# Spectral layer, soft mixture of experts and SoLU on one core: the turned slot weights kept slot-major, and the products with w_sb in another order

## The chip, the cores and the metric

The kernel runs on one core of a Trainium2 chip. The metric is the device time of one execution in microseconds; three runs of the kernel before took 1307.14, 1307.5 and 1311.27 us, and their median is 1307.5 us.

## The reference

All data are fp32. Three layers follow each other:

```
X = rfft(x, axis=1)                    # x: 8 batches x 3072 positions x 256
Yr, Yi = complex product of X with w_r, w_i, plus b_r, b_i
Yr, Yi = soft threshold at 0.01        # sign(y) * max(|y| - 0.01, 0)
x = irfft(Yr + i Yi)                   # flattened to 24576 x 256
logits = x @ phi                       # 32 slots
d = softmax of logits over all 24576 rows, c = softmax over the 32 slots
slot_input = d.T @ x                   # 32 x 256
slot_out = relu(slot_input @ w1[e]) @ w2[e]   # 8 experts, 4 slots each
x = c @ slot_out
h = x @ w_in; solu = h * softmax(h); ln = layernorm(solu) * g_ln
out = ln @ w_out
```

## The kernel before

The first stage (phase1) goes through the 8 batches. For each it transforms x, multiplies it with the weights of the frequencies (mix), thresholds, and keeps the result s in the frequency domain: 12 tiles of 128 x 512 per batch. The rows of the inverse transform are never formed. Because the transform is linear, logits and slot inputs are computed from s: the logits are the inverse transform of s @ phi (qt, qtr, e2, r_x, inv1), and the slot input of a batch is the forward transform of the weights d, multiplied with s.

That forward transform of d is the part that changes. Its steps for batch b are:

- fwd1 (two halves h): 16 small products per half give dt, 128 partitions (4 column groups l times 32 slots) by 8 x 4 x 32.
- dtr (two halves): four TensorE transposes of 128 x 128 per half write one PSUM tile, and ScalarE copies it to dm_sb, whose free axis is (position, l, slot).
- d_x (two halves z of 16 slots): VectorE's transpose of 32 x 32 blocks, dm_sb to dm2_sb, 128 x 512 each; input and output are read and written with the slot axis outermost and steps of 32 floats inside.
- fwd2: for each half c, products with w_sb (the tile w2_sb, 128 x 64 of it) into one PSUM tile of 128 x 384: columns of the array 0 to 63 write partitions 0 to 63, columns 64 to 127 write 64 to 127. The 32 columns of q = 0, t = 0 take another weight. ScalarE copies the tile to dh_sb.
- slots: 24 products of dh_sb with s, four column groups at a time, accumulate the slot input of the batch; acc takes it over the batches.

The order of the work is written out by hand. The main loop goes over the 96 tiles (b, t) and issues, for each, stage1 of a later tile, stage2 of the next one, st_transpose and mix. The steps above stand in a heap with a number of ticks behind their predecessor (LAG, and FAST for batch 6) and are issued between these parts, four ticks per tile. So each engine's queue is fixed when the kernel is built. Steps of a batch run while later tiles are being transformed. fwd2 of batches 0 to 6 is issued in this loop. For batch 7 nothing is left to run beside them, and the function last_chain writes its steps out one behind the other, with some filler matmuls on TensorE (run_on).

After it the second stage (phase2) computes the experts' outputs (first, turns, second) with weights that are loaded while last_chain runs, and then goes over 192 tiles of 128 rows: h, softmax, layer norm, and the product with w_out.

The helper mm issues every product (L89), tp every transpose (L92). An fp32 product is two matmul records and two weight loads in the trace, a transpose is one of each. In the names of the trace dm2_sb shows as dm_sb, r2_sb as r_sb, and the weight w2_sb as w_sb. The weight loads of inv_mm (r2, step of 32 floats) and of fwd_mm (d, contiguous), and the transposes in turns (h1, step of 8 floats) are read in the prediction beside the changed lines.

Of the kernel before, what the change touches and what calls it, by code (L numbers as in the profile page):

```python
# [13 lines left out]
AF = mybir.ActivationFunctionType  # L14
# [21 lines left out]
def kernel(  # L36
# [25 lines left out]
    PE, ACT, DVE, POOL, SP = nc.tensor, nc.scalar, nc.vector, nc.gpsimd, nc.sync  # L62
# [25 lines left out]
    def mm(out, lhsT, rhs, start=True, stop=True):  # L88
        PE.matmul(out=out, lhsT=lhsT, rhs=rhs, start=start, stop=stop)  # L89

    def tp(out, in_, k=128):
        PE.transpose(out=out, in_=in_, identity=ident[0:k, 0:k])  # L92
# [53 lines left out]
    def phase1(pl: ExitStack, pr_: ExitStack):  # L146
# [21 lines left out]
        w2_sb = ks_p.tile([128, 2, 2, 64], F32, name="w2_sb")  # L168
# [16 lines left out]
        def after(dq, fn, *a):  # L185
            heapq.heappush(heap, (now[0] + dq, now[1], fn, a))
            now[1] += 1
# [3 lines left out]
        def lag(name, b):  # L191
            return FAST[name] if b == B - 2 else LAG[name]
# [183 lines left out]
        small = {}  # L376
# [3 lines left out]
        def sm(name, shape, n=1):  # L380
            return sm_p.tile(shape, F32, name=name, tag=share.get(name, name), bufs=n)

        def pm(shape):
            return (small["pool"] if "pool" in small else psm).tile(shape, F32, name="pm", tag="pm")
# [71 lines left out]
        def r_x(b, z):  # L456
            if z == 0:
                small["r2", b] = sm("r2_sb", [128, 32, 32])
            sl = slice(16 * z, 16 * z + 16)
            DVE.transpose(out=small["r2", b][:, sl], in_=r_sb[:, sl])  # L460
            if z and b == B - 1:
                last_chain(b)
            elif z:
                after(lag("inv1", b), inv1, b, 0)
                after(lag("inv1", b) + 1, inv1, b, 1)

        def last_chain(b):
# [3 lines left out]
            dt = small["dt", b] = sm("dt_sb", [128, 8, 4, 32])  # L471
            POOL.memset(dt[:, :, :, 24:32], 0.0)
            pl_ = []
            for h in range(2):
                ps = pm([128, 4, 96])
# [14 lines left out]
            for h in range(2):  # L490
                ps = pm([96, 4, 128])
# [14 lines left out]
            for h in range(2):  # L506
                ps = pm([128, 4, 4, 24])
                fwd_mm(ps, d, h)
                ACT.activation(out=dt[:, 4 * h:4 * h + 4, :, 0:24], in_=ps, func=AF.Copy, scale=m3[:, 1 + h:2 + h])
            c = sm("c_sb", [96, 32, 32])  # L510
            rm, rs = sm("rm", [96, 32, 1]), sm("rs", [96, 32, 1])
            dm = small["dm", b] = sm("dm_sb", [128, 8, 128])
            for h in range(2):
                ps = pm([128, 4, 128])
                for k in range(4):
                    tp(ps[:, k, :], dt[:, 4 * h + k].rearrange("p c g -> p (c g)"))
                ACT.activation(out=dm[:, 4 * h:4 * h + 4, :], in_=ps, func=AF.Copy)
            lg = []
            for h in range(2):
                ps = psm.tile([96, 4, 128], F32, name="pm", tag="pm")  # L520
# [19 lines left out]
            DVE.tensor_scalar(out=srun, in0=srun, scalar1=m3[:, 0:1], scalar2=None, op0=ALU.mult)  # L540
            DVE.tensor_scalar(out=acc, in0=acc, scalar1=m3[:, 0:1], scalar2=None, op0=ALU.mult)
            d_x(b, 0)
            d_x(b, 1)
            for z in half:
                DVE.tensor_reduce(out=rm[:, z], in_=lg[z.start // 16], op=ALU.max, axis=AX.X)
                csub(z)
            fwd2(b)
            for z in half:
                cexp(z)
# [161 lines left out]
        def fwd1(b, h):  # L711
            if h == 0:
                small["dt", b] = sm("dt_sb", [128, 8, 4, 32])
                POOL.memset(small["dt", b][:, :, :, 24:32], 0.0)
            d, dt = small["d", b], small["dt", b]
            ps = pm([128, 4, 4, 24])
            fwd_mm(ps, d, h)
            ACT.activation(out=dt[:, 4 * h:4 * h + 4, :, 0:24], in_=ps, func=AF.Copy)
            after(LAG["dtr"], dtr, b, h)

        def dtr(b, h):
            if h == 0:
                small["dm", b] = sm("dm_sb", [128, 8, 128])
            dt, dm = small["dt", b], small["dm", b]
            ps = pm([128, 4, 128])
            for k in range(4):
                tp(ps[:, k, :], dt[:, 4 * h + k].rearrange("p c g -> p (c g)"))
            ACT.activation(out=dm[:, 4 * h:4 * h + 4, :], in_=ps, func=AF.Copy)
            if h == 1:
                after(lag("d_x", b), d_x, b, 0)  # L730
                after(lag("d_x", b) + 1, d_x, b, 1)

        def d_x(b, z):
            if z == 0:
                small["dm2", b] = sm("dm2_sb", [128, 32, 32])
            sl = slice(16 * z, 16 * z + 16)
            dm = small["dm", b].rearrange("p a (l s) -> p (a l) s", l=4)
            DVE.transpose(out=small["dm2", b].rearrange("p g s -> p s g")[:, sl], in_=dm.rearrange("p n s -> p s n")[:, sl])
            if z and b < B - 1:
                after(lag("fwd2", b), fwd2, b)  # L740

        def fwd2(b):
            dm2 = small["dm2", b][:, 0:24].rearrange("p (q g t) s -> p q g (t s)", q=3, g=2)
            dh = sm("dh_sb", [128, 2, NT, 32])
            for c in range(2):
                ps = pm([128, 3, 128])
                mm(ps[0:64, 0, 0:32], w2_sb[:, 1, c, :], dm2[:, 0, 0, 0:32])
                mm(ps[64:128], w2_sb[:, 0, c, :], dm2[:, :, 1, :])
                mm(ps[0:64, 0, 32:128], w2_sb[:, 0, c, :], dm2[:, 0, 0, 32:128])
                mm(ps[0:64, 1:3], w2_sb[:, 0, c, :], dm2[:, 1:3, 0, :])  # L750
                ACT.activation(out=dh[:, c].rearrange("p t s -> p (t s)"), in_=ps.rearrange("p q j -> p (q j)"), func=AF.Copy)
                small["dh", b] = dh
                if b == B - 1 and c == 0:
                    sums4(b)
            if 0 < b < B - 1:
                DVE.tensor_scalar(out=acc, in0=acc, scalar1=mexp[:, 0:1], scalar2=None, op0=ALU.mult)
            if b < B - 1:
                after(LAG["sums4"], sums4, b)
                after(LAG["slots"], slots, b)
# [37 lines left out]
        def sums4(b):  # L797
            s4 = sm("s4", [1, 4, 32])
            ACT.activation(out=s4, in_=small["dh", b][0:1, 0, 0:1, :].to_broadcast([1, 4, 32]), func=AF.Copy, scale=float(N))
            small["s4"] = s4  # L800
            if b < B - 1:
                after(LAG["sums"] + 2, sums, b, s4)
# [152 lines left out]
        for k in range(0, 8, 2):  # L955
            z = slice(128 * k, 128 * k + 256)
            decs.append((w_out[z].rearrange("(k p) d -> p k d", p=128), None, k))

        for i in range(B * NT):
            b, t = divmod(i, NT)  # L960
# [3 lines left out]
            if i + 1 < B * NT:  # L964
                stage2(*divmod(i + 1, NT))
                if t % 2 == 0:
                    k = i // 2 + 2
# [10 lines left out]
            if quiet:  # L978
                fn, a = quiet.pop(0)
# [9 lines left out]
        while heap or quiet:  # L989
            if quiet:  # L990
                fn, a = quiet.pop(0)
# [445 lines left out]
    with tc.manual_schedule():  # L1437
        with ExitStack() as ps_, ExitStack() as pl, ExitStack() as pw:
            s_p = ps_.enter_context(tc.tile_pool(name="s_p", bufs=NS))
            wa_p = pw.enter_context(tc.tile_pool(name="wa_p", bufs=2, side="right"))  # L1440
            g_p = pw.enter_context(tc.tile_pool(name="g_p", bufs=1, side="right"))
            gl = g_p.tile([128, 8], F32, name="gl")
            gm = g_p.tile([128, 1, D], F32, name="gm")
            with ExitStack() as pr_:
                steps = phase1(pl, pr_)
                next(steps)
            wb_p = pw.enter_context(tc.tile_pool(name="wb_p", bufs=15, side="right"))
            wi_p = pw.enter_context(tc.tile_pool(name="wi_p", bufs=1, side="right"))
            psg = pw.enter_context(tc.tile_pool(name="psg", bufs=1, space=PSUM, side="right"))
            wi = wi_p.tile([128, 2, DFF], F32R, name="wi")  # L1450
            load_w(wb_p, "wb", 15)
            SP.dma_start(out=wi.bitcast(F32), in_=win_dram.rearrange("(k p) f -> p k f", p=128))
            for _ in steps:
                pass
            pl.close()
            with ExitStack() as p2:
                phase2(p2, pw)
# [122 lines left out]
```

## Time and profile before

| | |
|---|---|
| median of three runs | 1307.5 us (1307.14 to 1311.27) |
| profiled execution | 1307.97 us, span 1306.2 us |
| granted TensorE clock, mean | 0.993 |
| busy: TensorE, VectorE, GpSimd, ScalarE | 97%, 86%, 77%, 76% |
| first stage | until about 597 us |
| tiles of the second stage | from about 622 us |

A group row of the profile gives line, engine, operation, the tiles written and read, the shape and the count. PE stands for TensorE's matmuls, PEld for its weight loads, DVE for VectorE, ACT for ScalarE, POOL for GpSimd, SP for the queue that issues most transfers. The duration of a matmul in the trace holds the way through the array as well, so matmuls that follow each other overlap in the trace; their rate is read from start to start.

### The profile page before, as it was taken

What the parts mean: (1) busy time and instruction counts of PE and PEld (TensorE: products, weight loads), DVE (VectorE), ACT (ScalarE), POOL (GpSimd) and SP (SyncE); (2) the same over time, 40 slices, a digit from 0 to 9 for tenths busy, and PEclk for the clock granted to TensorE, in tenths of its full rate; (3) what the DMA queues carried; (4) which work ended last, traced back from release to release, by engine and by line L of the source; (5) the groups of instructions that cost most, each with busy time, mean ns of one, the idle gap of its engine ahead of it and who ended that gap; (6) DMA issues with size and microseconds to landing.
All of it is one profiled execution on the core that took longest, in us unless ns stands there. A gap on an engine that the chain in (4) does not pass through costs nothing.

```text
span 1306.2 us, 30976 instructions
## 1 busy us (share of the span) xinstructions
PE 1263.1 (97%) x11042; PEld 1115.7 (85%) x11042; DVE 1127.9 (86%) x1568; ACT 988.0 (76%) x1831; POOL 1010.7 (77%) x1114
## 2 busy tenths in 40 slices
PE   6989999999999999899699999999999999999998
PEld 2867878787878878865699999999999999999998
DVE  1867887888788888765999999999999999999995
ACT  3545556565656565543799999999999999999996
POOL 0868686877778775433589999999999999998995
PEclk8999999999999999999999999999999999999999
DMA  8986465564747364259467777777777787777874
GB/s 269 279 229 191 125 176 165 142 198 122 203 118 223 100 200 144 93 186 351 99 168 203 194 192 208 178 196 195 187 203 180 185 229 191 187 198 178 211 180 127
DMA packets 181338, 241.79 MB, mean 185 GB/s; under 512 B 21984, under 2 KB 137056, under 8 KB 181184
## 3 DMA queue, kind: packets, MB, share of 16 engines
q1 hardware_dynamic: 180736, 238.62, 67.2%
q8 instruction: 88, 1.44, 0.5%
q10 hardware_dynamic: 448, 1.18, 0.3%
q14 instruction: 66, 0.54, 0.1%
HBM read 92.00 MB, written 59.11 MB: 116 GB/s over the span
## 4 chain that ended last, share of the span: by engine, by line
PE 82%; DVE 7%; DMA 3%; issue 2%; POOL 2%; ACT 2%; SPq 1%; DVEq 0%; ACTq 0%; POOLq 0%
PE po L89 37%; PE pb L89 9%; PE pm L89 8%; PE xps L89 7%; PE hps L89 6%; PE s L89 5%; PE pa L89 4%; PE sps L92 2%; DVE st L1167 2%; DVE u L1182 2%; PE hps L92 2%; DMA xc<-in_x_dram 1%; PE pm L92 1%; DMA t<-tb 1%; DVE tb L1205 1%
## 5 line engine op out<-in xcount | busy, mean ns | idle before, releaser
L1277 POOL TENSOR_TENSOR ul<-t,uh 128x512 fp32r<-128x512 f32 x336 | 431.2, 1301 | 43.4 <-ACT uh L1263 42.6
L89 PEld LDWEIGHTS po<-gw,uh 128*128 128x128 f32 x2736 | 347.3, 188 | 14.0
L89 PE MATMUL po<-gw,uh 128*128 128x256 f32 x2736 | 353.6, 280 | 0.0
L1167 DVE TENSOR_REDUCE st<-hps 128x1 f32<-128x1024 f32 x192 | 229.1, 1194 | 10.3 <-PE hps L89 10.3
L1182 DVE SCALAR_TENSOR_TENSOR u<-hps,e 128x1024 f32<-128x1024 f32 x192 | 232.1, 1209 | 0.5 <-ACT e L1174 0.3
L1174 ACT ACTIVATE e<-hps,st 128x1024 f32<-128x1024 f32 x192 | 215.4, 1122 | 16.8 <-DVE st L1167 16.8
L89 PE MATMUL po<-gw,ul 128*128 128x256 f32 x1620 | 228.1, 284 | 0.0
L1287 ACT ACTIVATE sq<-u,st 128x1024 f32<-128x1024 f32 x192 | 223.0, 1161 | 0.3 <-DVE u L1182 0.3
L1205 DVE STREAM_TRANSPOSE tb<-u 128x1024 f32<-128x1024 f32 x169 | 210.5, 1246 | 5.9
L89 PEld LDWEIGHTS po<-gw,ul 128*128 128x128 f32 x1620 | 206.1, 188 | 1.1
L350 POOL TENSOR_TENSOR s<-yb,s 128x512 f32<-128x512 f32 x95 | 124.4, 1310 | 103.9 <-DVE s L349 99.9
L1263 ACT ACTIVATE uh<-t 128x768 fp32r<-128x768 f32 x169 | 143.4, 849 | 0.0
L89 PEld LDWEIGHTS xps<-d_sb,apt 128*128 128x128 f32 x768 | 95.0, 194 | 54.7 <-issue 28.5
L89 PE MATMUL xps<-d_sb,apt 128*128 128x128 f32 x768 | 111.3, 288 | 11.8 <-DMA apt<-ad 7.8
L252 ACT ACTIVATE asb<-s 128x1024 f32<-128x1024 f32 x56 | 57.6, 1028 | 79.9 <-PE s L89 71.8
L89 PE MATMUL hps<-gst,ct 128*128 128x512 f32 x338 | 106.2, 396 | 7.5 <-DVE u L1182 6.1
L309 POOL TENSOR_TENSOR sl<-xsum,sh 128x256 fp32r<-128x256 f32 x93 | 78.0, 838 | 34.9 <-ACT sh L308 34.4
L225 POOL TENSOR_TENSOR x<-xc 112x512 f32<-112x512 f32 x56 | 72.1, 1288 | 39.8 <-DMA xc<-in_x_dram 37.0
L293 DVE TENSOR_TENSOR xsum<-xps,xi 128x256 f32<-128x256 f32 x96 | 39.8, 414 | 66.1 <-ACT xh L292 48.9
L1338 ACT ACTIVATE osb<-po,st 128x256 f32<-128x256 f32 x192 | 80.3, 475 | 8.3 <-PE po L89 4.5
L337 DVE TENSOR_TENSOR yb<-pb,bias 128x512 f32<-128x512 f32 x96 | 65.5, 683 | 18.6 <-PE pb L89 18.1
L349 DVE TENSOR_SCALAR s<-yb 128x512 f32<-128x512 f32 x95 | 75.2, 792 | 1.0
(237 smaller groups left out, 2375.6 us busy)
## 6 DMA issues: line engine op xcount, KB each, us to landing
t<-tb SPq DMA_DIRECT2D x676, 128.0 KB, 2.8
xc<-in_x_dram SPq DMA_DIRECT2D x128, 192.0 KB, 3.8
apt<-ad SPq DMA_DIRECT2D x96, 256.0 KB, 4.1
out_dram<-osb SPq DMA_DIRECT2D x47, 512.0 KB, 3.7
ad<-asb SPq DMA_DIRECT2D x112, 192.0 KB, 3.5
ct<-c_dram SPq DMA_DIRECT2D x96, 128.0 KB, 3.9
wt<-in_moe_w_dram SPq DMA_DIRECT2D x21, 512.0 KB, 9.0
ws<-in_moe_w_dram SPq DMA_DIRECT2D x22, 256.0 KB, 6.1
```

Of the source, the lines that this page charges most:

```text
L89: PE.matmul(out=out, lhsT=lhsT, rhs=rhs, start=start, stop=stop)
L309: (POOL if (b, t) > (0, 2) else DVE).tensor_tensor(out=sl, in0=sm_, in1=sh.bitcast(F32), op=ALU.subtract)
L349: DVE.tensor_scalar(out=s, in0=y, scalar1=-LAM, scalar2=LAM, op0=ALU.max, op1=ALU.min)
L350: POOL.tensor_tensor(out=s, in0=y, in1=s, op=ALU.subtract)
L1167: DVE.tensor_reduce(out=st[:, 0, k:k + 1], in_=hps[i], op=ALU.min, axis=AX.X)
L1174: ACT.activation(out=e, in_=hps[i], func=AF.Exp, bias=st[:, 0, k:k + 1], scale=-1.0, accum_out=st[:, 1, k:k + 1])
L1182: DVE.scalar_tensor_tensor(out=u, in0=hps[i] if turned(i) else hps.pop(i), scalar=1.0, in1=et.pop(i), op0=ALU.mult, op1=ALU.mult, accum_ou ...
L1205: DVE.transpose(out=t, in_=ut[i])
L1263: ACT.activation(out=w[:, 0:HA], in_=v[:, 0:HA], func=AF.Copy)
L1277: (DVE if n and i >= NI - 4 else POOL).tensor_tensor(out=ul[:, z, :].rearrange("p c (a j) -> p c a j", a=4), in0=v, in1=w.bitcast(F32), op ...
L1287: ACT.activation(out=sq, in_=ut.pop(i), func=AF.Square, bias=st[:, 2, k:k + 1], scale=-float(DFF), accum_out=st[:, 3, k:k + 1])
L1338: ACT.activation(out=o[:, k], in_=pot.pop(i), func=AF.Copy, scale=stt[j][:, 4, k:k + 1])
```

## The change

dm_sb is kept as (slot, position, l) and no longer as (position, l, slot). For this the four transposes of a half write their PSUM tile in the order slot, k, l, so the 128 columns of one transpose land in steps of 16 floats (runs of one float; l has a step of one float, slot of 16). ScalarE's copy reads the PSUM tile without gaps and writes, for each slot, 16 floats of dm_sb. The block transposes of d_x now read and write contiguous halves. dm2_sb stays in the order slot, position, and fwd2 reads it through a view: the moving operand of each product has the slot as its innermost axis with a step of 32 floats, before it had a step of one. The two long products are split by q: seven products per half c in place of four, with the halves of the array's columns alternating. The weights and the PSUM tile of fwd2 stay. The same helper, dt_turned, serves last_chain.

```diff
--- before.py
+++ after.py
@@ -509,12 +509,9 @@
                 ACT.activation(out=dt[:, 4 * h:4 * h + 4, :, 0:24], in_=ps, func=AF.Copy, scale=m3[:, 1 + h:2 + h])
             c = sm("c_sb", [96, 32, 32])
             rm, rs = sm("rm", [96, 32, 1]), sm("rs", [96, 32, 1])
-            dm = small["dm", b] = sm("dm_sb", [128, 8, 128])
+            small["dm", b] = sm("dm_sb", [128, 32, 32])
             for h in range(2):
-                ps = pm([128, 4, 128])
-                for k in range(4):
-                    tp(ps[:, k, :], dt[:, 4 * h + k].rearrange("p c g -> p (c g)"))
-                ACT.activation(out=dm[:, 4 * h:4 * h + 4, :], in_=ps, func=AF.Copy)
+                dt_turned(b, h)
             lg = []
             for h in range(2):
                 ps = psm.tile([96, 4, 128], F32, name="pm", tag="pm")
@@ -718,14 +715,16 @@
             ACT.activation(out=dt[:, 4 * h:4 * h + 4, :, 0:24], in_=ps, func=AF.Copy)
             after(LAG["dtr"], dtr, b, h)
 
+        def dt_turned(b, h):
+            ps = pm([128, 32, 4, 4])
+            for k in range(4):
+                tp(ps[:, :, k, :].rearrange("p s l -> p l s"), small["dt", b][:, 4 * h + k].rearrange("p c g -> p (c g)"))
+            ACT.activation(out=small["dm", b][:, :, 16 * h:16 * h + 16], in_=ps.rearrange("p s k l -> p s (k l)"), func=AF.Copy)
+
         def dtr(b, h):
             if h == 0:
-                small["dm", b] = sm("dm_sb", [128, 8, 128])
-            dt, dm = small["dt", b], small["dm", b]
-            ps = pm([128, 4, 128])
-            for k in range(4):
-                tp(ps[:, k, :], dt[:, 4 * h + k].rearrange("p c g -> p (c g)"))
-            ACT.activation(out=dm[:, 4 * h:4 * h + 4, :], in_=ps, func=AF.Copy)
+                small["dm", b] = sm("dm_sb", [128, 32, 32])
+            dt_turned(b, h)
             if h == 1:
                 after(lag("d_x", b), d_x, b, 0)
                 after(lag("d_x", b) + 1, d_x, b, 1)
@@ -734,20 +733,21 @@
             if z == 0:
                 small["dm2", b] = sm("dm2_sb", [128, 32, 32])
             sl = slice(16 * z, 16 * z + 16)
-            dm = small["dm", b].rearrange("p a (l s) -> p (a l) s", l=4)
-            DVE.transpose(out=small["dm2", b].rearrange("p g s -> p s g")[:, sl], in_=dm.rearrange("p n s -> p s n")[:, sl])
+            DVE.transpose(out=small["dm2", b][:, sl], in_=small["dm", b][:, sl])
             if z and b < B - 1:
                 after(lag("fwd2", b), fwd2, b)
 
         def fwd2(b):
-            dm2 = small["dm2", b][:, 0:24].rearrange("p (q g t) s -> p q g (t s)", q=3, g=2)
+            dm2 = small["dm2", b].rearrange("p s g -> p g s")[:, 0:24].rearrange("p (q g t) s -> p q g t s", q=3, g=2)
             dh = sm("dh_sb", [128, 2, NT, 32])
             for c in range(2):
                 ps = pm([128, 3, 128])
-                mm(ps[0:64, 0, 0:32], w2_sb[:, 1, c, :], dm2[:, 0, 0, 0:32])
-                mm(ps[64:128], w2_sb[:, 0, c, :], dm2[:, :, 1, :])
-                mm(ps[0:64, 0, 32:128], w2_sb[:, 0, c, :], dm2[:, 0, 0, 32:128])
-                mm(ps[0:64, 1:3], w2_sb[:, 0, c, :], dm2[:, 1:3, 0, :])
+                p4 = ps.rearrange("p q (t s) -> p q t s", t=4)
+                mm(p4[0:64, 0, 0:1], w2_sb[:, 1, c, :], dm2[:, 0, 0, 0:1])
+                for q in range(3):
+                    mm(p4[64:128, q], w2_sb[:, 0, c, :], dm2[:, q, 1])
+                    z = slice(1 if q == 0 else 0, 4)
+                    mm(p4[0:64, q, z], w2_sb[:, 0, c, :], dm2[:, q, 0, z])
                 ACT.activation(out=dh[:, c].rearrange("p t s -> p (t s)"), in_=ps.rearrange("p q j -> p (q j)"), func=AF.Copy)
                 small["dh", b] = dh
                 if b == B - 1 and c == 0:
```

## Rows read from the trace of the kernel before

**Rows 1.** The page's engine totals: busy us (share of the span) xinstructions.
```profile
PE 1263.1 (97%) x11042; PEld 1115.7 (85%) x11042; DVE 1127.9 (86%) x1568; ACT 988.0 (76%) x1831; POOL 1010.7 (77%) x1114
```

**Rows 2.** Stretches: each engine's busy us (xinstructions), granted clock, DMA share and rate.
```profile
core 0: us, PE busy (x) PEld busy (x) DVE busy (x) ACT busy (x) POOL busy (x), PEclk, DMA share, GB/s
165.00:230.00 65.00, 63.75 (x648) 52.49 (x641) 53.93 (x88) 39.99 (x80) 50.20 (x45) 1.00 0.62 171
360.00:425.00 65.00, 64.81 (x680) 52.06 (x679) 55.42 (x94) 38.56 (x80) 50.46 (x46) 1.00 0.61 171
```

**Rows 3.** Waits of TensorE's matmuls, 100 to 530 us: total us, times, longest us.
```profile
PE pm L89 <- DVE r_sb L460: 1.0, 1, 1.0
PE pm L92 <- ACT lg_sb L593: 1.0, 5, 0.2
```

**Rows 4.** By tile (dm_sb, r_sb, dt_sb, dh_sb): ns min/median/max, first and last start.
```profile
L738 DVE STREAM_TRANSPOSE dm_sb<-dm_sb x16: 1123/1147/1244, 154.7 to 590.9; 128x512 f32<-128x512 f32 x16
...
L460 DVE STREAM_TRANSPOSE r_sb<-r_sb x16: 661/696/710, 124.4 to 581.4; 128x512 f32<-128x512 f32 x16
...
L92 PE MATMUL pm<-ident,dt_sb x64: 272/273/328, 148.2 to 588.8; 128*128 128x128 f32 x64
L718 ACT ACTIVATE dt_sb<-pm x14: 465/491/493, 145.7 to 551.2; 128x384 f32<-128x384 f32 x14
...
L751 ACT ACTIVATE dh_sb<-pm x16: 464/492/522, 158.6 to 593.8; 128x384 f32<-128x384 f32 x16
```

**Rows 5.** Timeline of TensorE (start us, us): transposes of dt, h and u.
```profile
149.05 0.60 PE L92 MATMUL pm<-ident,dt_sb 128*128 128x128 f32 x4
...
608.84 1.16 PE L92 MATMUL pst<-ident,h 128*128 128x128 f32 x8
...
1283.58 1.06 PE L92 MATMUL pu<-ident,u 128*128 128x128 f32 x8 [0.67 <-DVE u L1182]
```

**Rows 6.** By tile (gst, h1t): ScalarE's reads of PSUM, ns min/median/max.
```profile
L1115 ACT ACTIVATE gst<-pg x2: 597/598/598, 619.0 to 620.4; 128x512 fp32r<-128x512 f32 x2
...
L1058 ACT ACTIVATE h1t<-pst x2: 597/597/597, 606.3 to 609.6; 128x512 f32<-128x512 f32 x2
```

**Rows 7.** Groups by form, at 228.64 us: count, busy us, mean ns.
```profile
L89 PE MATMUL pm<-dm_sb,w_sb 128*64 128x384 f32 x1 | 0.5, 486 | 0.0
L89 PE MATMUL pm<-dm_sb,w_sb 128*64 128x256 f32 x1 | 0.4, 379 | 0.0
```

**Rows 8.** Timeline of TensorE (start us, us): fwd2 of batch 1 and what follows.
```profile
227.43 1.64 PE L89 MATMUL pm<-dm_sb,w_sb 128*64 128x32 f32 x16
229.00 0.44 PE L92 MATMUL pm<-ident,qt_sb 128*128 128x128 f32 x2
```

**Rows 9.** By tile (r_sb, d_sb, dm_sb, pst, pu): weight loads, ns min/median/max.
```profile
L89 PEld LDWEIGHTS pm<-ft_sb,r_sb x512: 134/169/219, 127.0 to 583.5; 128*32 128x32 f32 x171
...
L89 PEld LDWEIGHTS pm<-f_sb,d_sb x512: 106/110/110, 143.3 to 587.4; 96*32 96x32 f32 x171
...
L89 PEld LDWEIGHTS pm<-dm_sb,w_sb x128: 132/137/138, 157.6 to 593.2; 128*64 128x64 f32 x128
...
L92 PEld LDWEIGHTS pst<-ident,h x16: 185/193/207, 605.6 to 609.6; 128*128 128x128 f32 x16
...
L92 PEld LDWEIGHTS pu<-ident,u x16: 138/140/143, 1283.5 to 1288.0; 128*128 128x128 f32 x16
```

**Rows 10.** Timeline of VectorE and of TensorE: d_x and fwd2 of batch 7.
```profile
589.84 2.16 DVE L738 STREAM_TRANSPOSE dm_sb<-dm_sb 128x512 f32<-128x512 f32 x2 [1.79 <-ACT dm_sb L517]
...
592.15 1.61 PE L89 MATMUL pm<-dm_sb,w_sb 128*64 128x32 f32 x16
```

**Rows 11.** Expert weights: SP's timeline, DMA issues to landing (us), TensorE's timeline.
```profile
607.79 1.49 SPq L123 DMA_DIRECT2D ws<-in_moe_w_dram  x2
...
ws<-in_moe_w_dram SPq DMA_DIRECT2D x2, 256.0 KB, 5.1
...
614.08 1.93 PE L89 MATMUL po<-ws,h1t 128*32 128x256 f32 x32
```

## The prediction

> **What bounds the kernel now.** I read the engine totals first, then the stretches, then TensorE's waits, then the timeline around the changed lines. TensorE is busy 97% of the span and VectorE 86% [rows 1]; the share alone doesn't say who waits. The stretch table does: in a 65 us stretch of the transform stage (batch 1 to 2, batch 4 to 5) TensorE is busy 63.75 and 64.81 us at full granted clock, while VectorE, ScalarE and GpSimd have 10 to 26 us free [rows 2]. The waits confirm it: from 100 to 530 us TensorE's matmuls wait 1.0 us for ScalarE's lg_sb and 1.0 us for VectorE's r_sb, each in all, and hardly for anything else [rows 3]. So in the loop over batches a nanosecond added to TensorE's queue is a nanosecond of time, and one saved on VectorE or ScalarE is worth nothing. The changed work runs once per batch: batches 0 to 6 in this loop, batch 7 in last_chain, where the steps wait for each other. The second stage of the kernel is only moved.
>
> **The change, part by part.** Three things move.
>
> *The block transposes on VectorE (d_x).* Two per batch, 128x512, at 1147 ns with 128-byte steps on both sides; the contiguous transpose of the same size in r_x takes 696 ns [rows 4]. I take 696, so 0.45 us less each, 7.2 us over 16. Fourteen of them run beside a full TensorE: nothing comes of them. If VectorE were on the path there it would be 6.3 us; the waits leave room for about 2.
>
> *The transposes of dt on TensorE and the copy behind them.* Same count, 8 per batch, 56 in the loop and 8 in last_chain; now each writes its 128 columns into PSUM in steps of 64 bytes. Four of them take 0.60 us in the timeline [rows 5], and one lasts 0.27 us [rows 4], so (0.60 - 0.27) / 3 = 109 ns from start to start. No row shows TensorE writing PSUM in steps. From below: ScalarE reads PSUM in 16-byte steps for gst at 597 ns for 512 elements, exactly what a contiguous h1t read takes [rows 6], so 0. From above: the columns stream at half rate. What 128 columns cost more at half rate shows in the weight load of h, 193 ns with a 32-byte step against 140 without for u [rows 9]: +53 ns each, 3.0 us over 56. Nearest is a TensorE row: the transposes of h (pst) read their weights in 32-byte steps and need 1.16 us for eight, the contiguous ones of u 1.06 [rows 5], 0.10 / 7 = about 15 ns each. I take 15 ns: +0.8 us over the 56. ScalarE's copy into dm now writes runs of 16 floats; its dt copy writes runs of 24 at 491 ns for 384 elements and its dh copy without gaps takes 492 [rows 4], so runs cost nothing and I leave the dm copy as it is.
>
> [...]
>
> *The products with w_sb (fwd2).* Per half c four products become seven, with the same columns: 384 for each half of the columns of the array. Every fp32 product is two instructions in the trace (16 rows for 8 products). Where no wait is in them, 384 columns take 486 ns and 256 take 379 [rows 7], 107 ns for 128, 0.83 ns a column, so 2 passes x 768 columns x 2 halves c = 3072 columns are 2.56 us one after the other. The stretch from the first product to the next instruction is 229.00 - 227.43 = 1.57 us [rows 8]. So the two column groups already run beside each other; the perfect overlap is 1.28 us, and the alternating order can win at most 0.29 us per batch, 2.0 us over seven. What is left over is weight loads in front of the short 32- and 96-column products, which stay short. I take 0 for the order.
>
> [...]
>
> What the change adds is the read: the moving operand, contiguous before, now has its 4-byte elements 128 bytes apart. No row has a moving operand like that. Lower bound: 0, if a column's 0.83 ns hides the slower read. Upper: the nearest row is a weight load with the very same 128-byte step, r_sb in inv_mm: 169 ns for 32 columns, against 110 for the contiguous load of d_sb in fwd_mm; a 64-column load takes 137 [rows 9], so 32 columns are 27 ns and with the step 27 + 59 = 86 ns. Four column groups load at once there. If each group pays by itself, that is 86 / 32 = 2.7 ns a column, 768 x 2 x 2.7 = 4.1 us per batch, +2.5 to +2.9 us. If the groups share one reader, it is 86 / 128 = 0.67 ns an element over all groups. The eight transposes of h speak for sharing: alone, with a 32-byte step, their 128-column load takes 193 ns against 140 [rows 9], 0.41 ns a column more, not 59 / 32 = 1.8. I take 0.67 ns: 3072 x 0.67 = 2.06 us, plus the 0.29 of loads, 2.35 us: +0.78 us per batch. Over seven batches: +5.5 us, all on TensorE, with nothing to hide it.
>
> *Batch 7.* Here the transposes are on the path: d_x starts at 589.84 after ScalarE's copy, takes 2.16 us, and the products start at 592.15 [rows 10]. They come 0.9 us earlier, then take 0.78 longer; the eight turned transposes cost 0.1. The sum is zero. Nor could a gain pass: the last two loads of expert weights are issued between 607.79 and 609.28 and land 5.1 us after their issue, so the last about 614, and the products with them start at 614.08 [rows 11]; the loads are queued one behind the other on SP, and no edit makes them earlier.
>
> **The sum.** +0.8 (transposes) + 5.5 (products) + 0 (batch 7) = +6.3 us. The profiled execution took 1307.97 us, its span 1306.2, so 1314.3 for it; the median of the three runs is 0.5 lower: 1313.8 us.
>
> **The rivals.**
> 1. *The steps are free* (not slower): a column of a two-pass product has 0.83 ns, twice what 53 ns for 128 transposed columns come to, so the reader has a spare turn for every element, and two groups have readers of their own. For it: the load of h with its step would fit (twice 0.41 ns a column). Against it: the load of r_sb, where four groups beside each other lose 59 ns. Then only the 56 transposes at 0 to 15 ns are left: 1307.5 to 1308.3 us. It decides as soon as an element costs under 0.42 ns over both groups.
> 2. *PSUM write at half rate, reads free*: 56 x 53 ns = +3.0, 1310.5 us. Together with the forecast's products it is 5.5 + 3.0, 1316.0 us, which I count into the forecast's case. [...]
> 3. *Every group pays the step by itself*: +2.7 us per batch, 19 us in the loop, and 2 in batch 7, where the products then outlast the 0.9 us won: about 1329 us. For it: the same step and 86 ns. Against it: the load of h.
> 4. *The order pays after all* (faster): steps free, and the 0.29 us of loads vanish: -2.0 in the loop, and 0.2 in batch 7, 1305.3 us.
>
> **How the numbers follow.** About 0.3% (3.9 us) is what a measurement of this kernel tells from no change: below 1303.6 is faster, above 1311.4 slower. Chances: the forecast, with the PSUM write anywhere between its bounds and the products at +0.5 to +1.2 us per batch, 0.50; rival 1 0.25; rival 2 0.10; rival 3 0.10; rival 4 0.05. Slower: nearly all of the forecast (0.46), rival 3 and a quarter of rival 2, together 0.58. Faster: part of rival 4 and chance, 0.04. The rest, 0.38, is no change. The range goes from 1306 (it leaves out rival 4 and the edge of rival 1) to 1322 (it leaves out rival 3). The forecast's own range is 1311 to 1317.5.
>
> **What would show it.** The stretch from the first product with w_sb to the next instruction: 2.35 us is right, 1.57 is rival 1, over 4 is rival 3, 1.28 is rival 4. Four transposes of dt: 0.64 us is right, 0.76 rival 2. The block transposes should fall to about 0.7 us with no gain in the loop. The forecast is wrong if the stretch doesn't grow, or if TensorE turns out to have waited for VectorE in the loop and the 65 us stretches get shorter.

## The result, and the profile after

The changed kernel took 1314.92 us (median of six runs, 1314.44 to 1317.84), the kernel before beside it 1307.64 us: ratio 1.006, 95% interval 1.0046 to 1.0074, so +6.0 to +9.7 us. It is slower by more than the 0.3% that a measurement can tell. Measured again later beside the kernel before (run "again" below), the ratio was 1.0072 (1.0058 to 1.0085), +9.4 us.

The engine totals of the profiled execution (span 1316.0 us), to be read against [rows 1]:

```profile
PE 1272.4 (97%) x11138; PEld 1123.2 (85%) x11138; DVE 1123.5 (85%) x1568; ACT 987.5 (75%) x1831; POOL 1011.6 (77%) x1114
```

TensorE has 96 instructions more (6 more products per batch, two records each, 8 batches) and 9.3 us more busy time; VectorE has 4.4 us less. The stretches and the waits of TensorE's matmuls from 100 to 530 us stand against [rows 2, 3]:

```profile
165.00:230.00 65.00, 63.76 (x651) 52.00 (x645) 52.11 (x85) 38.72 (x77) 50.23 (x45) 1.00 0.62 171
360.00:425.00 65.00, 64.81 (x658) 52.04 (x657) 53.18 (x91) 38.16 (x77) 50.27 (x45) 1.00 0.56 163
```

```profile
PE pm L89 <- DVE r_sb L460: 1.0, 1, 1.0
PE pm L92 <- ACT lg_sb L590: 1.0, 5, 0.2
PE pm L92 <- ACT qt_sb L420: 0.5, 1, 0.5
```

TensorE is as full as before and waits for the same things (the third line, which [rows 3] lack, was 0.8 us before). VectorE's busy time per stretch fell by 1.8 and 2.2 us, ScalarE's by 1.3 and 0.4. So the loop is longer because TensorE's queue is longer. Where, the timeline of TensorE shows, fwd2 of batch 1 as in [rows 8]:

```profile
228.28 2.83 PE L89 MATMUL pm<-dm_sb,w_sb 128*64 128x32 f32 x28
231.05 0.44 PE L92 MATMUL pm<-ident,qt_sb 128*128 128x128 f32 x2
```

From the first product to the next instruction it is now 2.77 us, before 1.57: +1.20 us per batch, 9.6 us over eight (the other batches differ from these by 0.03 us at most). One product, from the groups by form between 100 and 530 us (count, busy us, mean ns):

```profile
L89 PE MATMUL pm<-dm_sb,w_sb 128*64 128x128 f32 x120 | 17.0, 397 | 0.0
```

It lasts 397 ns. The two other things that the change touches, the turned transposes of dt against [rows 5] (timeline of TensorE), and the copy into dm_sb and the block transposes against [rows 4] (by tile):

```profile
148.77 0.60 PE L92 MATMUL pm<-ident,dt_sb 128*128 128x128 f32 x4
```

```profile
L722 ACT ACTIVATE dm_sb<-pm x16: 597/612/649, 148.9 to 597.3; 128x512 f32<-128x512 f32 x16
L736 DVE STREAM_TRANSPOSE dm_sb<-dm_sb x16: 665/698/712, 154.4 to 598.7; 128x512 f32<-128x512 f32 x16
```

The transposes cost exactly what they did, with a PSUM output in steps of 64 bytes; the block transposes fell from 1147 to 698 ns. In batch 7 the latter are done at 599.33 and nothing comes of it. On TensorE the chain of batch 7 is read from the transpose of mx, the maxima, to pslt, the products that turn the slot inputs for the experts. Before, against [rows 10], and after (timelines of TensorE and of VectorE):

```profile
584.73 0.27 PE L92 MATMUL pm<-ident,mx 128*1 128x128 f32 x1 [0.27 <-DVE mx L486]
...
591.11 1.05 PE L89 MATMUL idle<-ones 128*128 128x128 f32 x8
...
597.65 0.60 PE L89 MATMUL pslt<-sel,acc 128*128 128x32 f32 x4 [0.72 <-DVE acc L775]
```

```profile
592.92 0.27 PE L92 MATMUL pm<-ident,mx 128*1 128x128 f32 x1 [0.29 <-DVE mx L486]
...
598.03 1.30 DVE L736 STREAM_TRANSPOSE dm_sb<-dm_sb 128x512 f32<-128x512 f32 x2 [1.78 <-ACT dm_sb L722]
...
599.30 1.05 PE L89 MATMUL idle<-ones 128*128 128x128 f32 x8
600.28 2.83 PE L89 MATMUL pm<-dm_sb,w_sb 128*64 128x32 f32 x28
...
607.01 0.60 PE L89 MATMUL pslt<-sel,acc 128*128 128x32 f32 x4 [0.72 <-DVE acc L775]
```

The filler matmuls (idle) stand in TensorE's queue ahead of the products and run until 600.28. From the transpose of mx to the first product it is 7.36 us; before it was 7.42 (584.73 to 592.15). The 0.9 us that VectorE saved end as 0.06.

### The profile page after: what moved, and what is told of

It reads as the page before. It is cut to its first block, busy times and chain, and to the rows that moved or that the text cites. A ratio compares the mean times of both kernels' runs of the same rounds, so it can differ in the third digit from the quotient of the medians.

```text
span 1316.0 us, 31168 instructions
## 1 busy us (share of the span) xinstructions
PE 1272.4 (97%) x11138; PEld 1123.2 (85%) x11138; DVE 1123.5 (85%) x1568; ACT 987.5 (75%) x1831; POOL 1011.6 (77%) x1114
## 4 chain that ended last, share of the span: by engine, by line
PE 83%; DVE 7%; DMA 4%; ACT 2%; issue 2%; SPq 1%; POOL 1%; DVEq 0%; ACTq 0%; POOLq 0%
PE po L89 37%; PE pb L89 9%; PE pm L89 8%; PE xps L89 7%; PE hps L89 6%; PE s L89 5%; PE pa L89 4%; PE sps L92 2%; DVE u L1182 2%; DVE st L1167 2%; PE hps L92 2%; DMA xc<-in_x_dram 1%; PE pm L92 1%; DMA t<-tb 1%; DMA apt<-ad 1%
```

## The experiments

My theory after the result: the stepped read of the moving operand is the whole cost, because one of TensorE's two column groups is kept waiting while the other reads. Rivals: the six extra products or their order; the PSUM output in steps; a price that each group pays by itself. Each run below is compared by its fwd2 stretch of batch 1 on TensorE's timeline.

**order.** The kernel before, with only the seven products in place of its four:

```diff
...
+                p4 = ps.rearrange("p q (t s) -> p q t s", t=4)
+                mm(p4[0:64, 0, 0:1], w2_sb[:, 1, c, :], dm2[:, 0, 0, 0:1])
+                for q in range(3):
+                    mm(p4[64:128, q], w2_sb[:, 0, c, :], dm2[:, q, 1])
+                    z = slice(1 if q == 0 else 0, 4)
+                    mm(p4[0:64, q, z], w2_sb[:, 0, c, :], dm2[:, q, 0, z])
...
```

> The kernel before with its contiguous operand, only fwd2 split into the seven products in alternating order. If the stepped read is the whole cost (my theory), the stretch from the first product to the next instruction stays at 1.57 us or falls towards the 1.28 us of perfect overlap, and the time is that of before or up to 2.3 us less. If the cost lies in the six extra products or their order (rival), the stretch is near 2.77 us and the time near that of the changed kernel, +7 to +10 us.

```profile
225.63 1.65 PE L89 MATMUL pm<-dm_sb,w_sb 128*64 128x32 f32 x28
227.22 0.44 PE L92 MATMUL pm<-ident,qt_sb 128*128 128x128 f32 x2
```

1.59 us, and 1308.3 us against 1307.76 of before: ratio 1.0004 (0.9995 to 1.0012). Neither number nor order of the products costs anything, and the order wins nothing.

**runs4.** The changed kernel, t innermost in the operand, the step in the output:

```diff
-            dm2 = small["dm2", b].rearrange("p s g -> p g s")[:, 0:24].rearrange("p (q g t) s -> p q g t s", q=3, g=2)
+            dm2 = small["dm2", b][:, :, 0:24].rearrange("p s (q g t) -> p q g s t", q=3, g=2)
-                p4 = ps.rearrange("p q (t s) -> p q t s", t=4)
+                p4 = ps.rearrange("p q (t s) -> p q s t", t=4)
-                mm(p4[0:64, 0, 0:1], w2_sb[:, 1, c, :], dm2[:, 0, 0, 0:1])
+                mm(p4[0:64, 0, :, 0:1], w2_sb[:, 1, c, :], dm2[:, 0, 0, :, 0:1])
...
-                    mm(p4[0:64, q, z], w2_sb[:, 0, c, :], dm2[:, q, 0, z])
+                    mm(p4[0:64, q, :, z], w2_sb[:, 0, c, :], dm2[:, q, 0, :, z])
```

> The changed kernel, but the moving operand of fwd2 is read with t innermost (runs of 4 floats, 16 bytes) and the step sits in the PSUM output instead. If the price is per piece of 16 bytes that is read (my theory), the stretch is back at 1.57 us and the time at that of before, within 1 us, although VectorE's block transposes stay contiguous. If any step in the operand or in the PSUM output costs (rival), the stretch stays near 2.77 us.

```profile
225.78 1.65 PE L89 MATMUL pm<-dm_sb,w_sb 128*64 128x32 f32 x28
227.37 0.44 PE L92 MATMUL pm<-ident,qt_sb 128*128 128x128 f32 x2
```

1.59 us; 1306.81 against 1307.76 us, ratio 0.9992 (0.9983 to 1.0002). With runs of four floats the price is gone, though everything else of the change is in. (The short product of t = 0 still reads single floats 128 bytes apart; its 32 of 384 columns don't show in the stretch.) The PSUM output in steps of 128 bytes is free for products too, at their 0.83 ns a column. VectorE's shorter transposes (698 ns here) are worth nothing that can be measured.

**turn.** Only dt_turned and the slot-major dm_sb, with fwd2 and dm2_sb as before:

```diff
-            DVE.transpose(out=small["dm2", b][:, sl], in_=small["dm", b][:, sl])
+            DVE.transpose(out=small["dm2", b].rearrange("p g s -> p s g")[:, sl], in_=small["dm", b][:, sl])
...
```

> Only the first part of the change: dt's transposes write PSUM in steps and dm_sb is slot-major, d_x writes dm2_sb in steps as before, fwd2 is as before. Theory: four transposes of dt stay at 0.60 us, the products at 1.57 us, and the time is that of before within 1 us. Rival: the stepped PSUM write costs 15 to 53 ns a transpose, +1 to +3.4 us. d_x itself: 1.15 us if the stepped write sets its price, 0.70 us if the stepped read did.

By tile and on TensorE's timeline:

```profile
L736 DVE STREAM_TRANSPOSE dm_sb<-dm_sb x16: 1031/1068/1144, 153.7 to 591.2; 128x512 f32<-128x512 f32 x16
```

```profile
148.14 0.60 PE L92 MATMUL pm<-ident,dt_sb 128*128 128x128 f32 x4
...
226.56 1.64 PE L89 MATMUL pm<-dm_sb,w_sb 128*64 128x32 f32 x16
228.13 0.44 PE L92 MATMUL pm<-ident,qt_sb 128*128 128x128 f32 x2
```

1307.72 against 1307.76 us, ratio 1.0005 (0.9995 to 1.0015). The PSUM write in steps costs nothing, at the 109 ns from one transpose to the next. Of the 450 ns that d_x loses to its steps, the contiguous input wins back 79; the output makes the rest.

**onegroup.** The changed kernel, both halves on the same 64 columns of the array, so that one group works; the upper half of the result is left out:

```diff
-                    mm(p4[64:128, q], w2_sb[:, 0, c, :], dm2[:, q, 1])
+                    mm(p4[0:64, q], w2_sb[:, 0, c, :], dm2[:, q, 1])
...
-                ACT.activation(out=dh[:, c].rearrange("p t s -> p (t s)"), in_=ps.rearrange("p q j -> p (q j)"), func=AF.Copy)
+                for k in range(2):
+                    ACT.activation(out=dh[64 * k:64 * k + 64, c].rearrange("p t s -> p (t s)"), in_=ps[0:64].rearrange("p q j -> p (q j)"), func=AF.Copy)
```

> The changed kernel with all seven products of a half on columns 0 to 63 (the upper half of the result is left out), so that one reader is at work at a time. If both groups share one reader (theory), an element costs the same 0.85 ns alone, which 0.83 ns of column time nearly hides: stretch 2.6 to 2.9 us. If each group pays twice the time for a stepped column by itself (rival, 219 ns for 128 columns), the stretch is 5.2 to 5.5 us.

```profile
230.96 5.44 PE L89 MATMUL pm<-dm_sb,w_sb 128*64 128x32 f32 x28
236.32 0.44 PE L92 MATMUL pm<-ident,qt_sb 128*128 128x128 f32 x2
```

```profile
L89 PE MATMUL pm<-dm_sb,w_sb 128*64 128x128 f32 x120 | 30.0, 394 | 0.0
L89 PE MATMUL pm<-dm_sb,w_sb 128*64 128x96 f32 x24 | 6.1, 341 | 0.0
```

5.36 us, the rival's number: my theory of one shared reader falls. A 128-column product lasts 394 ns alone (second fence: by form, 100 to 530 us), as it does beside the other group (397). 32 columns more are 53 ns more, 1.66 ns a column; 3072 columns in 5.36 us are 1.74, loads included. That is twice the 0.83 ns of a contiguous column. The run also checks that the loop hides nothing: 1337.34 us is 29.6 us over 1307.76, and eight times 5.36 - 1.57 is 30.3.

**step2, step4, step8.** The changed kernel with each product's columns taken from dm2_sb in steps of 2, 4 or 8 floats (k; the operands are other elements of dm2_sb than the computation needs). The edit for k=2; with 4 and 8 the group on columns 64 to 127 starts at element 2 and 4:

```diff
...
+                flat = small["dm2", b].rearrange("p s g -> p (s g)").rearrange("p (n k) -> p k n", k=2)
+                mm(ps[0:64, 0, 0:32], w2_sb[:, 1, c, :], flat[:, 0, 0:32])
+                for q in range(3):
+                    mm(ps[64:128, q], w2_sb[:, 0, c, :], flat[:, 1, 0:128])
+                    z = 32 if q == 0 else 0
+                    mm(ps[0:64, q, z:128], w2_sb[:, 0, c, :], flat[:, 0, z:128])
...
```

> The changed kernel, but each product of fwd2 reads its columns from dm2_sb with a step of 2 floats (8 bytes; the values read are not those the reference needs). If what costs is a piece of 16 bytes that holds only one wanted element (theory), two fall into each piece: stretch 1.58 us. If any step other than one costs the double (rival), 2.77 us.

> As the run with a step of 2 floats, with a step of 4 floats (16 bytes). Theory of pieces of 16 bytes: 2.77 us, as with 128 bytes. Rival, that the price grows with the length of the step and only the long one costs: well under 2.77 us.

> As the run with a step of 2 floats, with a step of 8 floats (32 bytes). Theory of pieces of 16 bytes: 2.77 us. Rival, that the price grows with the length of the step: between the run with 4 floats and 2.77 us.

Step 2, step 4 and step 8, in this order:

```profile
226.55 1.70 PE L89 MATMUL pm<-dm_sb,w_sb 128*64 128x32 f32 x28
228.18 0.44 PE L92 MATMUL pm<-ident,qt_sb 128*128 128x128 f32 x2
```

```profile
228.08 2.96 PE L89 MATMUL pm<-dm_sb,w_sb 128*64 128x32 f32 x28
230.96 0.44 PE L92 MATMUL pm<-ident,qt_sb 128*128 128x128 f32 x2
```

```profile
229.50 2.99 PE L89 MATMUL pm<-dm_sb,w_sb 128*64 128x32 f32 x28
232.42 0.44 PE L92 MATMUL pm<-ident,qt_sb 128*128 128x128 f32 x2
```

1.63, 2.88 and 2.92 us (one run each: 1307.75, 1316.34 and 1318.68 us). Between 8 and 16 bytes the price appears, whole; from there to the 128 bytes of the change (2.77 us) it doesn't grow. This fits my theory of pieces of 16 bytes: with two wanted floats in a piece the stretch is 1.63 us, with one 2.88, with four (runs4) 1.59. But the size of the piece was my assumption, and the runs don't show it: no step between 8 and 16 bytes was run, so the steps alone don't tell such a piece from a limit on the length of the step. Against the length speaks runs4, where every fourth float is followed by a jump of 128 bytes and nothing is lost.

**best.** Runs4, without the fillers in front of fwd2 of batch 7:

```diff
             gmean(5, 8)
-            run_on(4)
```

> The run with runs of 4 floats, and in last_chain without the eight filler matmuls in front of fwd2 of batch 7. Theory: those fillers, not d_x, set the start of fwd2 there, so from the transpose of mx to the first product it falls from 7.37 to about 6.5 us; the products with the last expert weights then wait for their landing, so 0.2 to 0.9 us remain of it in the span. Rival: d_x or another step sets the start, and it stays at 7.37 us; or the clock falls and it is slower.

The waits of TensorE's matmuls from 587 to 605 us, the timelines of TensorE, VectorE and GpSimd, and the stretches (columns as in [rows 2]) there; ph are the experts' first products:

```profile
PE pslt L89 <- ACT sel L811: 1.4, 1, 1.4
```

```profile
581.43 0.27 PE L92 MATMUL pm<-ident,mx 128*1 128x128 f32 x1 [0.29 <-DVE mx L486]
...
587.99 1.62 PE L89 MATMUL pm<-dm_sb,w_sb 128*64 128x32 f32 x28
...
595.14 8.77 PE L89 MATMUL ph<-wt,slt 128*32 128x512 f32 x64 [0.36 <-ACT slt L1022]
```

```profile
591.40 1.79 DVE L532 TENSOR_SCALAR rs<-rs 96x16 f32<-96x16 f32 x1
...
594.65 0.17 DVE L532 TENSOR_SCALAR rs<-rs 96x16 f32<-96x16 f32 x1
```

```profile
588.47 4.70 POOL L788 TENSOR_TENSOR wo<-wo,gm 128x1024 f32<-128x1024 f32 x2 [15.43 <-ACT gm L785]
```

```profile
595.00:597.00 2.00, 1.86 (x12) 0.50 (x16) 0.78 (x2) 1.88 (x2) 1.08 (x2) 0.71 1.03 414
597.00:600.00 3.00, 3.00 (x24) 0.91 (x20) 1.40 (x2) 0.60 (x1) 3.00 (x1) 0.62 1.02 406
```

The first part held: the products come 6.56 us after the transpose of mx (581.43 to 587.99), so the fillers did set their start. Then it is lost twice. A small step of VectorE, which takes 0.17 us in the second half, lasts 1.79, and with it srun (the softmax's running sum) and sel, which is scaled with it, come late: pslt starts only 0.17 us earlier, counted from mx (12.74 against 12.91 in runs4).

The step ends with GpSimd's product of wo and gm: 593.19 and 593.17 us here, 594.43 and 594.40 in runs4, 596.51 and 596.47 in the kernel before (there the step lasts 0.97 and 0.95 us). In the changed kernel that product is over at 604.67, the step starts at 604.91, and it takes 0.17. In all four kernels the product ends 11.7 to 11.8 us after the transpose of mx, fillers or not. So this product on GpSimd, and not the fillers alone, seems to bound the chain; that the step waits for it is argued from these ends, and no run moves the product.

And after the 1.4 us wait of pslt the granted clock falls to 0.71 and 0.62 of full speed while the experts' first products run, and these take 8.77 us where they take 7.07 in runs4 and in the kernel before, at 1.00. 1307.72 against 1307.43 us, ratio 1.0003 (0.9993 to 1.0013): no gain.

**again and long.** The changed kernel once more; and runs4 with the short products last:

```diff
-                mm(p4[0:64, 0, :, 0:1], w2_sb[:, 1, c, :], dm2[:, 0, 0, :, 0:1])
-                for q in range(3):
+                for q in (1, 2, 0):
...
+                mm(p4[0:64, 0, :, 0:1], w2_sb[:, 1, c, :], dm2[:, 0, 0, :, 0:1])
```

> The changed kernel once more, beside the kernel before on the same chip, for a closer interval. If the 1.2 us per batch that the trace shows for the products is all there is and every nanosecond of it reaches the end (theory), the time is 9 to 10 us over that of before. If part of it is covered somewhere (rival), it stays at the 7.3 us of the first medians.

> The run with runs of 4 floats, with the 128-column products first and the 96- and 32-column ones last in each half. Theory: what is left over the 1.28 us of overlap are weight loads in front of short products, and behind long ones they are hidden: stretch 1.40 to 1.50 us, the time 0.6 to 1.4 us under the run with runs of 4 floats. Rival: the loads are not what is left, and it stays at 1.58 us.

```profile
227.90 1.65 PE L89 MATMUL pm<-dm_sb,w_sb 128*64 128x128 f32 x28
229.48 0.44 PE L92 MATMUL pm<-ident,qt_sb 128*128 128x128 f32 x2
```

"again": 1316.23 against 1307.68 us, ratio 1.0072 (1.0058 to 1.0085), +9.4 us by the ratio, close to the 9.6 us of the eight stretches. "long": 1.58 us, a miss; ratio 0.9992 (0.9983 to 1.0), the same as runs4. What the 0.3 us over perfect overlap are stays open: order doesn't move them.

No version here is measurably faster than the kernel before; runs4 and long come nearest to it, at 0.9992.

## Why the prediction was right, and which terms were off

The direction and the place were right: the loop is bound by TensorE [rows 2, 3], VectorE's saving is worth nothing there (runs4), and the price is the stepped read of fwd2's moving operand (order and turn without it: no change; runs4: gone). The predicted 1313.8 us lay 1.1 us under the first median and 2.4 us under the second. That it came so near is in part luck, since a cost that isn't there made up for some of one that was set too low. The terms:

- *Products, +0.78 us per batch.* Measured +1.20. The failing step is "If the groups share one reader, it is 86 / 128 = 0.67 ns an element over all groups", and the choice of it. They don't share (onegroup): each group pays about 1.7 ns for a column, twice 0.83. That is the mechanism of rival 3 at less than its 2.7 ns. The forecast came near it because 0.67 ns over both groups is 1.34 ns for a column of each, and by its own sign (2.35 us right, over 4 rival 3) 2.77 us would have counted for the forecast; only onegroup tells the two apart. The bounds, 0 and +2.5 to +2.9, held it. Nor was the weight load of r_sb [rows 9] a measure for it: the 2.7 ns a column of its upper bound is more than a moving column costs. Nearer was the load of h, which I used for the choice of reader but not for the size: it adds 0.41 ns to a column that takes about 0.44 without the step (96 columns of lt_sb load in 127 ns, 128 of dt_sb in 141), nearly the same factor.
- *Weight loads, 0.29 us kept beside the read.* Two passes of 768 columns in each group at 1.66 ns are 2.55 us, so 0.22 of the 2.77 are left, near what was kept.
- *Transposes of dt, +0.8 us.* Measured 0 (0.60 us for four before, after and in turn). ScalarE's stepped PSUM read [rows 6] was the right row, and the load of h the wrong one: there the step was in what TensorE reads, here in what it writes. Neither stepped output cost anything: 0.60 us for four transposes with 64-byte steps in turn, 1.59 us for the stretch with 128-byte steps in runs4, as in order without them.
- *Order of the products, 0.* Right: 1.57 us in the old order, 1.59 in the new one (order).
- *Batch 7, 0.* Measured +1.17 from mx to pslt (584.73 to 597.65 before, 592.92 to 607.01 after). The step that failed is "They come 0.9 us earlier": I took the end of d_x [rows 10] for the release of the products and passed over the fillers ahead of them on TensorE. The timeline before shows no gap between them (591.11 and 1.05 us) and the products (592.15), and that gap was the thing to look for. The other reason given, that the last expert weights let no gain pass, isn't borne out either: their last load is issued 24.2 us after the transpose of mx in the kernel before (608.9 us) and 22.2 us after it in runs4 (604.8), but the products with them start 29.3 us after it in both (614.08 and 611.98), and TensorE's waits from 575 to 640 us name no load in either.

The errors were of both signs: 8 x 1.20 = 9.6 us in all, where I had 5.5 for seven batches, 0.8 for transposes and 0 for batch 7.

## What to carry to other kernels

Before a layout change moves a step from one engine to another, look which engine is full: here 0.9 us of VectorE per batch, which had time, were bought with 1.2 us of TensorE. Give a moving operand runs or short steps where you can: here runs of four floats and steps of 8 bytes cost nothing (1.59 and 1.63 us for the stretch), and single floats 16 to 128 bytes apart made it 2.77 to 2.92 us. The step could go into the PSUM output instead, where it was free in both forms tried (0.60 us for four transposes, 1.59 us for the stretch). When an engine becomes ready earlier in a chain, look at what is queued ahead of its consumer, fillers included, and at which other engine the chain meets next, before counting a gain.

## What the runs showed of the hardware

- Moving fp32 operand, two-pass product: 0.83 ns a column in steps of 4 bytes [rows 7], about the same in steps of 8 (1.63 us for the stretch in step2, 1.59 contiguous in order), 1.7 ns in steps of 128 (onegroup), and about the same in steps of 16 and 32 (2.88 and 2.92 us in step4 and step8, 2.77 after the change); each of two column groups pays by itself (a 128-column product takes 394 ns alone, 397 beside the other group).
- A PSUM output in steps of 64 bytes (transposes) or 128 bytes in its inner axis (products) costs TensorE nothing measurable, at 109 ns a transpose (four in 0.60 us, turn) and 0.83 ns a column (stretch of 1.59 us, runs4); no run has such an output at a faster rate.
- VectorE's 128x512 block transpose: 698 ns contiguous, 1068 with a stepped output, 1147 with both sides stepped.
- Without the eight filler matmuls, and with a TensorE wait of 1.4 us after the products, the granted clock was 0.71 and 0.62 in the two stretches behind the wait, and 64 products took 8.77 us; with them, and a wait of 0.7 us, 1.00 and 7.07 us.
- VectorE's step on rs (96x16) took 0.17 us with GpSimd idle (changed kernel), and 0.95 to 1.79 us when it began beside GpSimd's 128x1024 products: it ended 0.02 to 0.04 us after them in the kernel before, runs4 and best.
